# A fused attention and two-layer MoE kernel: the first token block's maximum is spread 14 instead of 4 scheduling steps behind the block's load

## The chip, the core and the metric

The kernel runs on one core of a Trainium2 chip. The core has five engines with a queue each: TensorE (PE in the profile, its weight loads PEld), VectorE (DVE), ScalarE (ACT), GpSimd (POOL) and SyncE (SP), which issues all the DMAs that matter here. Each engine works through its own queue in order and waits on semaphores for the others. The metric is the device time of one execution in microseconds (us), the median of several runs.

## What is computed

Attention with RMS-normalized q and k (batch 4, 12 heads, 448 tokens, head size 64), then two MLPs on the 1792 x 768 result:

```python
def _attn_ref(q, k, v, g_q, g_k):
    q_n, k_n = (rmsnorm(q, g_q), rmsnorm(k, g_k))
    scores = scale * np.matmul(q_n, k_n.transpose(0, 1, 3, 2))
    attn = softmax(scores)
    return np.matmul(attn, v)

def _moe_ref(x, w_in, w_out):            # 768 -> 2048 -> 768
    h = x @ w_in
    g = h * (1.0 / (1.0 + np.exp(-1.702 * h)))
    return g @ w_out

def _moe2_ref(x, w_in, w_out, alpha):    # 768 -> 2048 -> 768
    h = x @ w_in
    g = np.maximum(h, 0.0) + alpha * np.minimum(h, 0.0)
    return g @ w_out
```

(`softmax` stands for the reference's subtraction of the row maximum, exponential and division by the sum.) Large matmuls run as three float16 products of a high and a low half (high x high, high x low, low x high), so every operand is first scaled by a power of two into float16's range and then split in two by `split`: ScalarE writes the high half, VectorE the low half.

## The kernel before

The program has two layers. In the first, attention and the first MLP of the four batches b = 0 to 3 are interleaved. The last part of batch 3 is `moe1_out` (line 680): six output slices j of 128 rows, each one PSUM tile `yp` that 48 matmuls (line 689, 128x448) accumulate; ScalarE then copies it out (`y`, line 697) and SP stores it to `y_dram` (line 698). Below, one such run of 48 matmuls is called a **y group**. Its tiles come from the PSUM pool `ps_m` with three buffers, which small helpers also use.

While batch 3 runs, the generator `late_weights` (line 953) is advanced next to it: it loads and splits the second layer's input weights `w2i` (lines 963 to 966, with a last call of `weight_scales`, which spreads the weights' maximum over the partitions), then opens the pools of the second layer and calls `prepare(0)` (line 735). `prepare` works on a block of tokens, 512 for block 0, in two steps:

- first step: load the block of the first layer's output, `yr`, from `y_dram` (line 740), take each partition's largest absolute value on VectorE (`yone`, line 742), round it to a power of two (lines 104 and 105);
- second step: `partition_max` (line 114) makes a diagonal `diag` of these values (line 117), a single 128x128 matmul with a matrix of ones spreads them over the partitions (`pm`, line 119), VectorE takes the maximum (`my`, line 120); from it follow the scales `ysc` (line 752), the split of the block into its two halves `x2` (lines 124 and 125, six slices) and a factor `co` (line 757).

Between the two steps `late_weights` yields `P0` times (lines 971 and 972). The loop of lines 1097 to 1106 advances it once for a tick of `moe1` in the first 32 ticks, and twice for a tick after that; one y group has four ticks. What is left when the ticks are over is run out by `second_layer` (line 977) at its start. The yields thus decide which y groups are written ahead of the second step. A scheduler that orders by the written place then fixes each engine's queue.

`yr` lies in memory that the weights' staging tiles held, so its load waits for the last split of `w2i` on VectorE (line 164). Behind the y groups stand, on TensorE, the small matmul for `alpha`'s maximum (`partition_max` at line 726, tile `a`), and then the second layer's first product (line 774, `h`), which reads `x2` and `w2i`. The loads of the second layer's output weights (line 808) wait for the last y group, since they take over `g`'s memory.

Of the kernel before, what the change touches and what calls it, by code (L numbers as in the profile page):

```python
# [46 lines left out]
G1I = 1  # L47
G1O = 2
P1 = (2, 8)
P0 = 4  # L50
PAIR0 = 44
W2_RAW = 6
RSQRT_SEED = float(0x5F3759DF)
# [3 lines left out]
def attention_moe_kernel(  # L57
# [895 lines left out]
    def late_weights(ctx, att):  # L953
# [16 lines left out]
        next(first)  # L970
        for _ in range(P0):
            yield
# [165 lines left out]
```

## Time and profile before

| | us |
|---|---|
| median of 3 runs | 1230.93 (1230.83 to 1232.2) |
| the profiled execution | 1225.37 |
| its span, first to last instruction | 1223.6 |
| TensorE busy in it | 1088.8 |
| VectorE busy in it | 837.8 |
| ScalarE busy in it | 708.2 |

The page gives one profiled execution. Times in the trace count from the span's start. A busy TensorE is not TensorE at its peak, since its matmuls overlap; idle time in front of a matmul is a plainer sign, and the trace names what ended it. The granted TensorE clock stands as a share: 1.00 is 2.4 GHz, 0.50 is 1.2 GHz.

### The profile page before, as it was taken

Reading aid. Unit: us, or ns where it says so; the run is one execution under the profiler, and the core shown is the slowest. Engines: PE = TensorE matmul, PEld = TensorE weight load, DVE = VectorE, ACT = ScalarE, POOL = GpSimd, SP = SyncE. Lnnn points to the kernel's source line nnn. Section 1 sums busy time; section 2 is a strip of 40 time slices with the busy share of each in tenths; the row PEclk is TensorE's granted clock in tenths of the full one; section 3 lists DMA queues with packets and bytes.
Section 4 is the critical chain, followed back from the end, with each engine's and each line's share of the span. In section 5 each row is a group of like instructions: output and inputs, shape, how many; then the busy total and the mean of one; then the engine's idle time right before and its main releaser. Section 6 shows DMA issues by size and latency. Waiting matters only on the chain.

```text
span 1223.6 us, 18355 instructions
## 1 busy us (share of the span) xinstructions
PE 1088.8 (89%) x6685; PEld 616.3 (50%) x6685; DVE 837.8 (68%) x1602; ACT 708.2 (58%) x1465; POOL 79.4 (6%) x56
## 2 busy tenths in 40 slices
PE   0557698887999998999999998599999999999998
PEld 0334466665554444555555544244444467666665
DVE  7989888988656887466741858439896343787441
ACT  3656687888468687567852545126666444565220
POOL 0000000112311222020000000000000000000000
PEclk9968699999999999999999999799999999999999
DMA  8994446388678887666651821356524215353100
GB/s 205 248 263 139 112 130 166 68 169 145 145 153 155 140 168 151 146 131 119 121 102 47 312 73 50 118 191 221 204 88 155 78 65 165 94 166 108 55 33 33
DMA packets 300010, 166.11 MB, mean 136 GB/s; under 512 B 238736, under 2 KB 283280, under 8 KB 299920
## 3 DMA queue, kind: packets, MB, share of 16 engines
q1 hardware_dynamic: 299920, 164.95, 53.2%
q8 instruction: 52, 0.85, 0.3%
q14 instruction: 38, 0.31, 0.1%
HBM read 92.02 MB, written 25.69 MB: 96 GB/s over the span
## 4 chain that ended last, share of the span: by engine, by line
PE 55%; DVE 18%; DMA 12%; ACT 8%; issue 5%; SPq 3%; DVEq 0%; ACTq 0%
PE op L930 16%; PE yp L689 14%; PE hp L666 7%; PE h L774 7%; PE xp L516 5%; PE sp L438 3%; DVE ph L493 2%; DMA yr<-y_dram 2%; DMA g<-in_moe_w_in_dram 2%; PE tp L485 2%; DMA pt<-ph 2%; PE hp L619 1%; DMA t<-hl 1%; DVE g L125 1%; ACT pr L452 1%
## 5 line engine op out<-in xcount | busy, mean ns | idle before, releaser
L689 PE MATMUL yp<-g,w1o 128*128 128x448 f16 x1152 | 227.9, 357 | 0.6 <-DVE g L125 0.4
L774 PE MATMUL h<-x,w2i 128*128 128x512 f16 (+1 forms) x1152 | 219.3, 352 | 2.6 <-ACT neg L781 2.5
L666 PE MATMUL hp<-x,w1i 128*128 128x448 f16 x864 | 169.5, 353 | 4.4 <-DVE t L675 4.4
L774 PEld LDWEIGHTS <-w2i 128*128 128x128 f16 x1152 | 112.6, 98 | 108.1 <-issue 3.5
L689 PEld LDWEIGHTS <-w1o 128*128 128x128 f16 x1152 | 111.8, 99 | 109.6 <-issue 10.2
L666 PEld LDWEIGHTS <-w1i 128*128 128x128 f16 x864 | 82.9, 98 | 84.7 <-issue 8.9
L452 ACT ACTIVATE pr<-sp,nm,c_s 128x448 f32<-128x448 f32 x168 | 120.3, 720 | 2.5 <-PE tp L485 0.6
L493 DVE SCALAR_TENSOR_TENSOR ph<-pr,sm,ph 128x448 f16<-128x448 f32 x126 | 98.1, 805 | 20.4 <-ACT ph L470 19.5
L443 DVE TENSOR_REDUCE nm<-sp 128x2 f32<-128x896 f32 x96 | 92.7, 966 | 26.6 <-PE sp L438 26.3
L930 PEld LDWEIGHTS <-even 128*128 128x128 f16 x672 | 65.7, 98 | 43.1
L470 ACT ACTIVATE ph<-pr,sm 128x448 f16<-128x448 f32 x126 | 77.7, 659 | 12.9 <-DVE sm L461 9.6
L782 DVE SCALAR_TENSOR_TENSOR pos<-neg,nalpha,pos 128x512 f32<-128x512 f32 (+1 forms) x64 | 43.4, 679 | 60.0 <-ACT neg L781 59.8
L780 ACT ACTIVATE pos<-h 128x512 f32<-128x512 f32 (+1 forms) x64 | 34.4, 538 | 72.6 <-PE h L774 60.0
L619 PE MATMUL hp<-x,w1i 128*128 128x192 f16 (+1 forms) x576 | 60.3, 259 | 8.3 <-DVE t L631 3.9
L930 PEld LDWEIGHTS <-odd 128*128 128x128 f16 x504 | 49.3, 98 | 32.6
L438 PE MATMUL sp<-w1o 128*128 128x448 f16 (+1 forms) x64 | 21.4, 468 | 48.2 <-DMA w1o<-hl 31.5
L438 PE MATMUL sp<-t 128*128 128x448 f16 (+1 forms) x160 | 53.2, 377 | 12.2 <-ACT pr L452 8.1
L930 PE MATMUL op<-w2lo,even 128*128 128x384 f16 x384 | 63.5, 326 | 0.0
L444 ACT ACTIVATE nm<-nm,c_s 128x2 f32<-128x2 f32 x96 | 27.9, 291 | 56.2 <-DVE nm L443 55.9
L619 PEld LDWEIGHTS <-w1i 128*128 128x128 f16 x576 | 51.8, 98 | 16.3 <-issue 10.6
L485 PE MATMUL tp<-dg,pr 128*128 128x128 f32 x336 | 49.8, 301 | 10.3 <-DVE dg L465 7.6
L438 PE MATMUL sp<-t,t 128*128 128x448 f16 (+1 forms) x160 | 52.6, 374 | 6.7 <-DMA t<-t 6.7
(202 smaller groups left out, 1686.9 us busy)
## 6 DMA issues: line engine op xcount, KB each, us to landing
g<-in_moe_w_in_dram SPq DMA_DIRECT2D x24, 512.0 KB, 5.8
g<-in_moe_w_out_dram SPq DMA_DIRECT2D x32, 384.0 KB, 4.0
w2raw<-in_moe_w_in_dram SPq DMA_DIRECT2D x24, 512.0 KB, 5.6
w2raw<-in_moe_w_out_dram SPq DMA_DIRECT2D x16, 768.0 KB, 6.7
g_dram<-pos SPq DMA_DIRECT2D x48, 256.0 KB, 2.0
gp<-g_dram SPq DMA_DIRECT2D x8, 1024.0 KB, 7.4
odd<-g_dram SPq DMA_DIRECT2D x6, 1024.0 KB, 5.6
qk<-in_q_dram SPq DMA_DIRECT2D x24, 224.0 KB, 3.6
```

The lines of the kernel that those rows point to most:

```text
L438: nc.tensor.matmul(out=sp[rows, i, 0:S], lhsT=t1[:, c, rows], rhs=kt[:, j * S:(j + 1) * S], start=(e == 0), stop=(e == 1))
L443: nc.vector.tensor_reduce(out=nm[:, 0:n], in_=sp[:, 0:n, 0:S], op=ALU.max, axis=AX, negate=True)
L452: nc.scalar.activation(out=pr[i], in_=sp[:, i, 0:S], func=AF.Exp, bias=nm[:, i:i + 1], scale=c_s, accum_out=sm[:, i:i + 1])
L470: nc.scalar.activation(out=ph[:, i, 0:S], in_=pr[i], func=AF.Copy, scale=sm[:, i:i + 1])
L485: nc.tensor.matmul(out=tp[:, c, i], lhsT=pr[i][:, o:o + 128], rhs=ph[:, i], start=True, stop=True)
L493: nc.vector.scalar_tensor_tensor(out=ph[:, i, S:2 * S], in0=pr[i], scalar=sm[:, i:i + 1], in1=ph[:, i, 0:S], op0=ALU.mult, op1=ALU.subtract)
L516: nc.tensor.matmul(out=xp[64 * j:64 * j + 64, t:t + n], lhsT=vs[ks, c, j], rhs=pt[ks, kc, o:o + n], start=(i == 0), stop=(i == len(steps) ...
L619: nc.tensor.matmul(out=ps, lhsT=w1i[:, kk, e, m * 128:(m + 1) * 128], rhs=xs[0, kk][:, f, cols], start=(i == 0), stop=(i == 3 * KD - 1))
L666: nc.tensor.matmul(out=ps, lhsT=w1i[:, kk, e, m * 128:(m + 1) * 128], rhs=x[:, f], start=(n == 0), stop=(n == 3 * KD - 1))
L689: nc.tensor.matmul(out=ps, lhsT=w1o[:, m, e, j * 128:(j + 1) * 128], rhs=g[:, m, f], start=(n == 0), stop=(n == 3 * KF - 1))
L774: nc.tensor.matmul(out=ps, lhsT=w2i[:, kk, e, m * 128:(m + 1) * 128], rhs=x2[kk][:, f], start=(c == 0), stop=(c == 3 * KD - 1))
L930: nc.tensor.matmul(out=ps, lhsT=ops[:, o, m, f], rhs=rhs[:, e], start=(c == 0), stop=(c == 3 * KH - 1))
```

## The change

One number changes. The second step of `prepare(0)` is written ten more steps of `late_weights` later.

```diff
-P0 = 4
+P0 = 14
```

No instruction is added or removed. On TensorE's queue the place is the end of the `w2i` work and the middle of batch 3's y groups. In the names, `pm_7906` spreads the maximum of `w2i`, `pm_7954` that of token block 0, and `yp_7888` and `yp_7996` are two y groups. Before:

```order
L689 MATMUL yp_7888<-g_7233,w1o_78 128x448
L119 LDWEIGHTS ones_75 [waits DVE_49]
L119 MATMUL pm_7906<-diag_7904,ones_75 128x128 [waits Activation_49]
L119 LDWEIGHTS ones_75 [waits DVE_49]
L119 MATMUL pm_7954<-diag_7952,ones_75 128x128 [waits Activation_49]
L689 LDWEIGHTS w1o_78
L689 MATMUL yp_7996<-g_7233,w1o_78 128x448 [waits Activation_49]
```

The two small matmuls stand next to each other, and three y groups (144 matmuls) follow. With the change, at the same place of TensorE's queue, a y group (`yp_7966`) comes right behind the first small matmul:

```order
L689 MATMUL yp_7888<-g_7233,w1o_78 128x448
L119 LDWEIGHTS ones_75 [waits DVE_49]
L119 MATMUL pm_7906<-diag_7904,ones_75 128x128 [waits Activation_49]
L689 LDWEIGHTS w1o_78
L689 MATMUL yp_7966<-g_7233,w1o_78 128x448 [waits Activation_49]
```

and the small matmul of token block 0 (now `pm_8021`) stands behind that group's 48 matmuls, still on TensorE's queue:

```order
L689 MATMUL yp_7966<-g_7233,w1o_78 128x448
L119 LDWEIGHTS ones_75 [waits DVE_49]
L119 MATMUL pm_8021<-diag_8019,ones_75 128x128 [waits Activation_49]
L689 LDWEIGHTS w1o_78
L689 MATMUL yp_8048<-g_7233,w1o_78 128x448
```

So the small matmul has moved past one y group; two groups are left behind it instead of three. On ScalarE's queue the copy of that group (`y_8015`) has moved ahead of the six first halves of block 0, of which two are shown:

```order
L697 ACTIVATE y_7963<-yp_7888,c_y_99 128x448 [waits DMAHW7_49,PE_49,Activation_49]
L697 ACTIVATE y_8015<-yp_7966,c_y_99 128x448 [waits DMAHW0_49,PE_49,Activation_49]
L124 ACTIVATE x2_8028<-yr_7921,ysc_8026 128x512 [waits DMAHW2_49,DVE_49,Activation_49]
L124 ACTIVATE x2_8029<-yr_7921,ysc_8026 128x512
L124 ACTIVATE x2_8030<-yr_7921,ysc_8026 128x512
```

Before, that copy stood behind the six. On SP's queue the group's store has moved ahead of the load of token block 1 (`yr_8267`), behind that of block 0 (`yr_7921`):

```order
 L698 DMA y_dram_72<-y_7883 128x448 [waits Activation_49]
-L698 DMA y_dram_72<-y_7993 128x448 [waits DMAHW1_49,Activation_49]
+L698 DMA y_dram_72<-y_7963 128x448 [waits DMAHW1_49,Activation_49]
 L740 DMA yr_7921<-y_dram_72 128x6x512 [waits DMAHW4_49,DMAHW5_49,DMAHW3_49,DMAHW6_49,DMAHW2_49,DVE_49]
+L698 DMA y_dram_72<-y_8015 128x448 [waits Activation_49]
 L740 DMA yr_8267<-y_dram_72 128x6x512 [waits DMAHW2_49,DVE_49]
-L698 DMA y_dram_72<-y_8045 128x448 [waits Activation_49]
 L698 DMA y_dram_72<-y_8097 128x448 [waits Activation_49]
```

One store has passed one load there. VectorE's queue and GpSimd's have the same instructions in the same order, with other buffer numbers.

## Rows read from the trace of the kernel before

**Rows 1.** Page, part 1: busy us (share of span) and instructions by engine
```profile
PE 1088.8 (89%) x6685; PEld 616.3 (50%) x6685; DVE 837.8 (68%) x1602; ACT 708.2 (58%) x1465; POOL 79.4 (6%) x56
```

**Rows 2.** Waits of PE, whole span: us in total, times, longest
```profile
PE sp L438 <- DMA w1o<-hl: 31.5, 2, 27.4
PE pm L119 <- DVE diag L117: 19.7, 2, 16.8
```

**Rows 3.** Timeline, PE alone: start, us, engine line op, [idle before <-releaser]
```profile
61.81 4.88 PE L485 MATMUL tp<-dg,pr 128*128 128x128 f32 x24 [6.67 <-DVE dg L465]
...
760.31 0.22 PE L119 MATMUL pm<-diag,ones 128*128 128x128 bf16 x1
777.37 0.29 PE L119 MATMUL pm<-diag,ones 128*128 128x128 bf16 x1 [16.84 <-DVE diag L117]
777.45 30.01 PE L689 MATMUL yp<-g,w1o 128*128 128x448 f16 x144
807.30 0.22 PE L119 MATMUL pm<-diag,ones 128*128 128x128 bf16 x1
```

**Rows 4.** Timeline, ACT alone, 748 to 835 us
```profile
752.92 0.61 ACT L697 ACTIVATE y<-yp,c_y 128x448 f32<-128x448 f32 x1
...
763.72 0.61 ACT L697 ACTIVATE y<-yp,c_y 128x448 f32<-128x448 f32 x1
778.57 3.78 ACT L124 ACTIVATE x<-yr,ysc 128x512 f16<-128x512 f32 x6 [14.23 <-DVE ysc L752]
...
798.47 0.63 ACT L697 ACTIVATE y<-yp,c_y 128x448 f32<-128x448 f32 x1 [8.50 <-PE yp L689]
807.55 0.63 ACT L697 ACTIVATE y<-yp,c_y 128x448 f32<-128x448 f32 x1 [8.45 <-PE pm L119]
```

**Rows 5.** Timeline, all engines, 755 to 835 us: the chain of block 0
```profile
764.42 2.34 DVE L164 SCALAR_TENSOR_TENSOR w2i<-w2n,inv_w2i,w2i 128x2048 f16<-128x2048 f32 x1
...
766.79 16.99 SPq L740 DMA_DIRECT2D yr<-y_dram  x2
...
773.29 3.35 DVE L742 TENSOR_REDUCE yone<-yr 128x1 f32<-128x3072 f32 x1 [6.00 <-DMA yr<-y_dram]
...
777.05 0.25 DVE L117 TENSOR_SCALAR diag<-ident,yone 128x128 bf16<-128x128 bf16 x1
...
777.69 0.29 DVE L120 TENSOR_REDUCE my<-pm 128x1 f32<-128x128 f32 x1 [0.38 <-PE pm L119]
...
779.32 4.06 DVE L125 SCALAR_TENSOR_TENSOR x<-yr,ysc,x 128x512 f16<-128x512 f32 x6 [0.84 <-ACT x L124]
...
789.91 3.35 DVE L742 TENSOR_REDUCE yone<-yr 128x1 f32<-128x3072 f32 x1 [6.53 <-DMA yr<-y_dram]
...
807.76 0.24 DVE L117 TENSOR_SCALAR diag<-ident,yone 128x128 bf16<-128x128 bf16 x1
```

**Rows 6.** Busy time by stretch: us, each engine (instructions), PEclk, DMA share, GB/s
```profile
61.81:65.93 4.12, 4.12 (x19) 4.12 (x20) 4.12 (x11) 0.68 (x1) 0.00 (x0) 0.50 0.97 307
266.66:270.59 3.93, 0.00 (x0) 0.10 (x1) 3.93 (x8) 3.58 (x10) 0.00 (x0) 1.00 0.93 187
270.59:274.14 3.55, 3.55 (x26) 2.28 (x27) 3.55 (x10) 3.55 (x11) 1.05 (x1) 0.52 0.62 129
760.53:765.66 5.13, 0.00 (x0) 0.00 (x0) 3.71 (x3) 3.80 (x3) 0.00 (x0) 1.00 0.09 35
765.66:777.37 11.71, 0.01 (x1) 0.01 (x1) 5.47 (x8) 0.00 (x0) 0.00 (x0) 0.50 0.40 139
777.37:782.73 5.36, 5.36 (x16) 2.26 (x17) 4.20 (x11) 3.78 (x6) 0.00 (x0) 0.50 0.00 0
```

**Rows 7.** DMA issues, 762 to 775 us: count, KB each, median us to landing
```profile
yr<-y_dram SPq DMA_DIRECT2D x1, 1536.0 KB, 6.5
y_dram<-y SPq DMA_DIRECT2D x1, 224.0 KB, 1.9
```

**Rows 8.** Waits of PE, 807.6 us to the span's end
```profile
PE h L774 <- ACT neg L781: 2.5, 3, 1.7
```

## The prediction

> **What bounds the kernel now.** I read the engines' busy shares first: TensorE 89%, VectorE 68%, ScalarE 58% [rows 1]. TensorE is the engine to follow, but a share does not say where the time of one edit goes, so I went on to TensorE's waits. The largest is the start-up (27.4 us in one stop); the next largest single stop is 16.8 us, of the small matmul `pm` for the diagonal that VectorE makes [rows 2]. The timeline puts that stop at the edited place: the weights' `pm` ends at 760.31 + 0.22 = 760.53, block 0's `pm` starts at 777.37, and 144 matmuls of three y groups queue behind it [rows 3]. Those matmuls need nothing of block 0; they stand still only because TensorE's queue is in order.
>
> What ends the stop is block 0's chain, in the order of time [rows 5]: the last split of `w2i` ends at 766.76 and frees the staging memory; the load of `yr` is issued at 766.79 (the row merges it with block 1's load) and VectorE starts the maximum at 773.29; that takes 3.35, two small steps follow, and `diag` ends at 777.30. No step of this chain uses TensorE, so it is neither sped up nor held by what TensorE does meanwhile.
>
> Behind the y groups TensorE hardly waits: 2.5 us in the remaining 416 us of the span [rows 8]. So time gained on TensorE in this place should last to the end.
>
> **What the change moves, and its price.** Nothing is added or removed, and the small matmul passes one y group.
>
> *The y group in the hole.* A group at full clock is read from the copies of two successive groups, both of which wait for their group and start at 798.47 and 807.55 [rows 4]: 9.08 us. 144 matmuls took 30.01 [rows 3], where 3 x 9.08 = 27.24 would be the full-clock time; the surplus, 2.8 us, is the clock (below). The group can start right at 760.53: its PSUM tile is the one three requests back in a pool of three, whose copy ended at 752.92 + 0.61 = 753.53 [rows 4]. It then ends at 760.53 + 9.08 = 769.61. If it had to wait for the newer copy, which ends at 764.33 [rows 4], it would end at 773.4. Both are before 777.30, so the gain is the same: TensorE's stop shrinks from 16.84 to 7.76 us in the first case, `pm` stays at 777.37, and 96 matmuls are left behind it instead of 144. The gain is **9.08 us**.
>
> *The clock.* In the old stop the clock went from 1.00 to 0.50 at 765.66, 5.13 us into it, and after work resumed it stayed at 0.50 for 5.36 us [rows 6]. At half the rate that costs half of the stretch, 2.7 us, which agrees with the surplus of 2.8. Will a stop of 7.76 us still cost it? The two nearest stops are shorter, and both did: one of 6.67 us before 61.81 [rows 3] was followed by 4.12 us at 0.50, and one of 3.93 us before 270.59 [rows 6] by 3.55 us at 0.52. So the fall stays, and only its length varies: half of 3.55 to 5.36 us is 1.8 to 2.7. Against the 2.7 of now that is 0 to 0.9 us of further gain; I take 0, from the row of the same work (y groups), and keep 0.9 for the range.
>
> The Trainium skill, page "TensorE: Matmul & The Clock Gate" (section "Part 1: The HAM clock gate"), says that the number of slow matmuls at one place differs from run to run, and warns against fitting to one count. By it, the 5.36 us of this one execution are no fixed price and the clock term could come out somewhat longer too; no row here repeats the same place.
>
> *The group's copy.* On ScalarE it is now ahead of block 0's six first halves. It runs at about 769.6 for 0.6 us, in what was an idle stretch of 14.23 us before 778.57 [rows 4]; cost nothing. If the group ended only at 773.4 it would still fit.
>
> *The group's store.* SP issues it at about 770.3, behind block 0's load, which then is in flight until about 773.3. Before, no other transfer ran beside that load: the previous store could be issued when its copy had ended at 764.33 [rows 4], and landed in 1.9 us [rows 7]. If the two share the engines evenly, the load loses the store's share, 224 / 1536 x 6.5 = 0.95 us [rows 7], and `pm` and all behind it come that much later; if the store's packets wait their turn, nothing. Below nothing is excluded: a store does not speed a load. I take 0, since the load's packets were all queued 3.5 us earlier, and keep 0.95.
>
> The Trainium skill, page "DMA: Bandwidth & Descriptors" (section "Issuing engines are not separate DMA queues"), says that all DMAs run on the same 16 engines and interleave. By that rule the gain here would be 9.08 - 0.95 = 8.1 us instead of 9.1; no row of the kernel before has this pair in flight.
>
> *What SP's store passes.* Block 1's load stands behind it on SP and waits for block 0's split in any case, which ends at 783.38 [rows 5]; the store is issued 13 us before. No cost.
>
> *What is late next.* Block 0's split stays at 778.57 to 783.38 [rows 4, 5]. The last y group ends 9.1 us earlier, near 798.4; then come `alpha`'s small matmul and the second layer. Its inputs are there since 783.4. Block 1's `diag` waited behind `alpha`'s maximum until 807.76; its own maximum ended near 793.3 [rows 5], so it has 5 us to spare when everything moves up. The output weights' loads wait for the last y group, so they move up with it. Nothing becomes the new bound.
>
> **The sum.** Span 1223.6 - 9.1 = 1214.5; profiled execution 1225.37 - 9.1 = 1216.3. The median of the runs is 5.6 us above the profiled execution; I carry the difference over: 1230.93 - 9.1 = **1221.8 us**. With the bounds (0.95 lost, 0.9 gained) the forecast's own range is 1220.9 to 1222.8.
>
> **Rivals.**
> (a) The shorter stop does not drop the clock, and the surplus of 2.8 goes too: 9.1 + 2.8 = 11.9, 1219.0 us. For it: the stop is less than half as long. Against it: a stop of 3.93 us was enough [rows 6].
> (b) The gain is given back later, because the second layer's first 100 us hang on the output weights or on VectorE and not on TensorE: 1230.9. For it: VectorE is busy 68% overall [rows 1]. Against it: TensorE waits 2.5 us behind the place [rows 8], and the weights' loads move up as well.
> (c) Slower, by the clock: TensorE's busy time is now cut in two by the stop, and if the low level lasted through both remaining groups, 96 matmuls would take 4 x 9.08 = 36.3 us. From 760.53 on: 9.08 + 7.76 + 36.3 = 53.2, against 16.84 + 30.0 = 46.9 now: 6.3 us slower, 1237.2. It decides from a low stretch of 5.36 + 2 x 9.08 = 23.5 us on. Against it: the three low stretches after dense work resumed are 3.55, 4.12 and 5.36 us [rows 6].
> (d) The change does not do what it says, since the scheduler could have put the instructions where they were: excluded by the queues shown with the change, so I give it no chance.
>
> **How the numbers follow.** Forecast 0.84, (a) 0.05, (b) 0.05, (c) 0.02, and 0.04 for a part of the gain given back (1223.5 to 1228). A measurement of this kernel can tell about 0.2%, 2.5 us. Faster by more than that: the forecast, (a) and most of the partial case, 0.92; within 0.2%: (b) and the rest, 0.06; slower: 0.02. The range: the forecast's 1220.9 to 1222.8, widened by the 1.4 us that the three runs span, and down to (a): 1219.0 to 1224.2, which I round up to 1224.4.
>
> **What would show it.** In the profile of the changed kernel TensorE's wait for `diag` should be 7.8 us long (7 to 9); a y group of 9.1 us should lie directly behind the weights' `pm`; block 0's `pm` should start within 1 us of 777.4; the clock should read 0.50 for some 3.5 to 5.5 us behind it; block 0's load should land 6.5 to 7.4 us after its issue; `alpha`'s `pm` should start near 798.2 and everything behind it 9 us earlier than now, to the last store. Wrong would be: a `pm` that moves with the group (then the chain of block 0 does hang on TensorE), full clock behind the stop (a), or new waits of line 774 that eat the gain (b).

## The result, and the profile after

The changed kernel takes 1220.39 us (median of 4 runs, 1219.69 to 1220.57), the kernel before 1230.99 (4 runs, 1230.83 to 1232.2). By the medians that is 10.6 us faster. The ratio is 0.9911, 95% interval 0.9894 to 0.9928, or 11.0 us, between 8.9 and 13.0. Forecast were 1221.8 us, 9.1 us below, and a range of 1219.0 to 1224.4.

The profiled execution of the changed kernel took 1220.57 us with a span of 1218.8. That is only 4.8 us less than the span before; where the other 6 us are, the first experiment shows. First the edited place.

Timeline of the changed kernel, TensorE alone (start, duration, line and operation, idle time before and what ended it); it answers to [rows 3]:

```profile
766.44 0.23 PE L119 MATMUL pm<-diag,ones 128*128 128x128 bf16 x1 [0.57 <-DVE diag L117]
766.50 9.24 PE L689 MATMUL yp<-g,w1o 128*128 128x448 f16 x48
783.60 0.29 PE L119 MATMUL pm<-diag,ones 128*128 128x128 bf16 x1 [7.86 <-DVE diag L117]
783.68 20.24 PE L689 MATMUL yp<-g,w1o 128*128 128x448 f16 x96
803.76 0.22 PE L119 MATMUL pm<-diag,ones 128*128 128x128 bf16 x1
803.81 35.13 PE L774 MATMUL h<-x,w2i 128*128 128x512 f16 x162
```

The y group (48 matmuls) stands directly behind the weights' small matmul, the stop has shrunk from 16.84 to 7.86 us, and two groups (96 matmuls) are left behind it. The chain of block 0 in the same stretch, timeline of all engines, which answers to [rows 5]:

```profile
770.57 2.34 DVE L164 SCALAR_TENSOR_TENSOR w2i<-w2n,inv_w2i,w2i 128x2048 f16<-128x2048 f32 x1
...
772.94 0.37 SPq L740 DMA_DIRECT2D yr<-y_dram  x1
...
775.83 0.64 ACT L697 ACTIVATE y<-yp,c_y 128x448 f32<-128x448 f32 x1 [5.35 <-issue]
776.50 0.32 SPq L698 DMA_DIRECT2D y_dram<-y  x1
779.53 3.35 DVE L742 TENSOR_REDUCE yone<-yr 128x1 f32<-128x3072 f32 x1 [6.09 <-DMA yr<-y_dram]
...
783.29 0.25 DVE L117 TENSOR_SCALAR diag<-ident,yone 128x128 bf16<-128x128 bf16 x1
...
784.80 3.78 ACT L124 ACTIVATE x<-yr,ysc 128x512 f16<-128x512 f32 x6 [8.33 <-DVE ysc L752]
```

It runs as before, 6.1 to 6.2 us later as a whole. From the weights' small matmul to block 0's it is 783.60 - 766.44 = 17.16 us, before 777.37 - 760.31 = 17.06 [rows 3]. The moved copy (775.83) and the moved store (776.50) lie inside the chain's wait for its load. Busy time and clock by stretch (us, then PE, PEld, DVE, ACT, POOL busy with counts, PEclk, DMA share, GB/s), which answers to [rows 6]:

```profile
766.67:775.74 9.07, 9.07 (x48) 4.50 (x46) 5.27 (x6) 3.81 (x3) 0.00 (x0) 1.00 0.24 65
775.74:780.72 4.98, 0.01 (x1) 0.00 (x0) 1.19 (x1) 0.64 (x1) 0.00 (x0) 1.00 0.75 290
780.72:783.60 2.88, 0.00 (x0) 0.00 (x1) 2.72 (x4) 0.00 (x0) 0.00 (x0) 0.50 0.00 0
783.60:787.55 3.95, 3.95 (x12) 1.73 (x13) 2.78 (x8) 2.75 (x5) 0.00 (x0) 0.50 0.00 0
```

The group ran at full clock; the clock fell 4.98 us into the stop and stayed at 0.50 for 3.95 us after it, where it had stayed for 5.36. The wait of TensorE behind the place (807.6 us to the end before [rows 8], 804 us to the end now) and the two transfers that meet (KB, median us to landing; before [rows 7]) are:

```profile
PE h L774 <- ACT neg L781: 1.6, 1, 1.6
```

```profile
yr<-y_dram SPq DMA_DIRECT2D x1, 1536.0 KB, 6.6
y_dram<-y SPq DMA_DIRECT2D x1, 224.0 KB, 3.6
```

The stretch from the weights' small matmul to alpha's is 803.76 - 766.44 = 37.32 us against 807.30 - 760.31 = 46.99: 9.67 us gained. From alpha's small matmul to the end of the span it is 415.0 us against 416.3: another 1.3. That makes 11.0, near the measured 10.6. The stretch starts 6.1 us later (766.44 instead of 760.31), so the two spans differ by 4.8 us only.

### The profile page after: what moved, and what is told of

Its sections match the earlier page's. It is cut to its first block, busy times and chain, and to the rows that moved or that the text cites. A ratio compares the mean times of both kernels' runs of the same rounds, so it can differ in the third digit from the quotient of the medians.

```text
span 1218.8 us, 18355 instructions
## 1 busy us (share of the span) xinstructions
PE 1092.8 (90%) x6685; PEld 618.4 (51%) x6685; DVE 838.6 (69%) x1602; ACT 709.5 (58%) x1465; POOL 79.8 (7%) x56
## 4 chain that ended last, share of the span: by engine, by line
PE 54%; DVE 17%; DMA 13%; ACT 8%; issue 5%; SPq 3%; POOL 0%; ACTq 0%; DVEq 0%
PE op L930 16%; PE yp L689 13%; PE hp L666 7%; PE h L774 7%; PE xp L516 5%; PE sp L438 3%; DVE ph L493 2%; DMA qk<-in_q_dram 2%; DMA yr<-y_dram 2%; DMA w1o<-hl 2%; PE tp L485 2%; PE hp L619 2%; ACT pr L452 2%; DMA w2raw<-in_moe_w_in_dram 2%; DVE nm L443 1%
## 5 line engine op out<-in xcount | busy, mean ns | idle before, releaser
L493 DVE SCALAR_TENSOR_TENSOR ph<-pr,sm,ph 128x448 f16<-128x448 f32 x126 | 98.7, 810 | 19.1 <-ACT ph L470 18.2
L619 PE MATMUL hp<-x,w1i 128*128 128x192 f16 (+1 forms) x576 | 63.7, 268 | 8.3 <-DVE t L631 3.9
L619 PEld LDWEIGHTS <-w1i 128*128 128x128 f16 x576 | 53.5, 101 | 17.8 <-issue 10.6
```

Source lines behind the costliest of these rows:

```text
L493: nc.vector.scalar_tensor_tensor(out=ph[:, i, S:2 * S], in0=pr[i], scalar=sm[:, i:i + 1], in1=ph[:, i, 0:S], op0=ALU.mult, op1=ALU.subtract)
L619: nc.tensor.matmul(out=ps, lhsT=w1i[:, kk, e, m * 128:(m + 1) * 128], rhs=xs[0, kk][:, f, cols], start=(i == 0), stop=(i == 3 * KD - 1))
```

## The experiments

**The hole theory.** The chain of block 0 needs about 17.1 us from the weights' small matmul to block 0's, whatever TensorE does. What TensorE can do of the y groups in this time is the gain. The rest of the time it stands (the hole), and behind a long stop it pays for the low clock in addition. Its rivals: the gain comes from the clock; it comes from the first part of the program or from the second layer; or what was moved ahead of the chain stretches it.

All profiles together. "Weights' pm" is the start of that small matmul, "to block 0's pm" the chain, "stop" TensorE's idle time in front of the latter, "low clock" the time at 0.50 behind the stop, "to alpha's pm" the stretch in which the change lies, "rest" what follows up to the end of the span. All in us. Two rows are not like the others: with the useless fill ten matmuls of the fill stand ahead of the weights' small matmul, and with three groups alpha's small matmul stands right behind block 0's, ahead of the second layer's new wait.

| kernel | weights' pm | to block 0's pm | stop | low clock | to alpha's pm | rest |
|---|---|---|---|---|---|---|
| before | 760.31 | 17.06 | 16.84 | 5.36 | 46.99 | 416.3 |
| before, again | 762.29 | 17.12 | 16.90 | 6.02 | 47.38 | 415.5 |
| after | 766.44 | 17.16 | 7.86 | 3.95 | 37.32 | 415.0 |
| after, again | 760.48 | 16.81 | 7.51 | 5.13 | 37.54 | 415.7 |
| two groups | 766.08 | 18.22 | none | none | 27.35 | 413.1 |
| two groups, again | 762.64 | 18.22 | none | none | 27.36 | 413.1 |
| useless fill | 770.82 | 15.76 | 0.75 | none | 43.07 | 415.9 |
| three groups | 764.92 | 27.30 | none | none | 28.06 | 416.9 |

### The kernel before, profiled once more

No edit.

> The kernel before, unchanged, profiled once more. Question: the profile of the changed kernel reaches the weights' small matmul at 766.4 us, the one of before at 760.3, although the program up to there is the same. Theory A (executions differ in the first part by themselves): the matmul starts anywhere from 759 to 768 us here, while the stretch from it to alpha's small matmul is 46.5 to 47.9 us as before (46.99), with a stop of 16.7 to 17.0 us. Rival B (the change makes the first part 6 us longer and gives 6 us more back elsewhere): the matmul starts at 760 to 761 us again.

Timeline, TensorE alone, and the stretch at the low clock behind the stop:

```profile
762.29 0.22 PE L119 MATMUL pm<-diag,ones 128*128 128x128 bf16 x1
779.41 0.29 PE L119 MATMUL pm<-diag,ones 128*128 128x128 bf16 x1 [16.90 <-DVE diag L117]
779.49 30.34 PE L689 MATMUL yp<-g,w1o 128*128 128x448 f16 x144
809.67 0.22 PE L119 MATMUL pm<-diag,ones 128*128 128x128 bf16 x1
```

```profile
779.41:785.43 6.02, 6.02 (x17) 2.50 (x18) 4.85 (x11) 3.79 (x6) 0.00 (x0) 0.50 0.00 0
```

The weights' small matmul is at 762.29, 2 us later than in the first profile; the stretch is 47.38 us. So the part ahead of the edit differs by itself from execution to execution, and not in step with the edit: the changed kernel reached the place at 760.48 in its second profile, and all eight profiles, with the same order of instructions up to there, at 760.3 to 769.1 (the latest is the useless fill's, where the end of the y group ahead is the mark). Theory A holds. The spread comes early: the windows of the first 100 us show the clock at different levels on average, here in the kernel before (760.31), in the changed one (766.44) and in the changed one again (760.48):

```profile
0.00:100.00 100.00, 40.96 (x179) 23.22 (x180) 84.70 (x191) 51.91 (x100) 0.79 (x8) 0.85 0.91 232
```

```profile
0.00:100.00 100.00, 41.60 (x167) 22.80 (x168) 83.34 (x191) 50.82 (x97) 0.80 (x8) 0.83 0.88 226
```

```profile
0.00:100.00 100.00, 40.28 (x178) 23.23 (x179) 84.58 (x191) 51.85 (x99) 0.79 (x8) 0.88 0.89 231
```

In the late execution TensorE has got through 167 matmuls in that time, in the two early ones through 179 and 178, at a higher clock. It is not the whole of it: the execution with most, 184 at 0.88, is the second profile of the kernel before, and it came to the place at 762.29. That the clock is the cause was not tested; it may as well be the consequence of later loads. What follows for reading: spans of single executions can differ by up to 9 us here for this reason alone, so the spans cannot be compared, but the stretch between two marks can.

### The changed kernel once more

No edit; the times stand beside the experiments of the same chip.

> The changed kernel once more, for times beside the others and for a second look at the clock. Hole theory (a y group fills the stop, the chain of block 0 keeps its length): the stretch from the weights' small matmul to alpha's is 36.6 to 38.3 us, with a stop of 7.7 to 8.0 us; what varies is the low-clock stretch behind the stop, which was 3.95 us and was 5.36 in the kernel before. Time about 1220.4. Rival (the lower time comes from the first part or the second layer): the stretch differs from the first profile by more than 1 us while the time stays.

1219.12 us, ratio to the kernel before 0.9932 (0.9906 to 0.9958). Timeline of TensorE, the stretch behind the stop, and the two diagonals that VectorE makes for the weights and for block 0:

```profile
760.48 0.22 PE L119 MATMUL pm<-diag,ones 128*128 128x128 bf16 x1
760.53 9.24 PE L689 MATMUL yp<-g,w1o 128*128 128x448 f16 x48
777.29 0.29 PE L119 MATMUL pm<-diag,ones 128*128 128x128 bf16 x1 [7.51 <-DVE diag L117]
777.37 20.82 PE L689 MATMUL yp<-g,w1o 128*128 128x448 f16 x96
798.02 0.22 PE L119 MATMUL pm<-diag,ones 128*128 128x128 bf16 x1
```

```profile
777.29:782.42 5.13, 5.13 (x15) 2.21 (x16) 3.97 (x10) 3.78 (x6) 0.00 (x0) 0.50 0.00 0
```

```profile
759.59 0.25 DVE L117 TENSOR_SCALAR diag<-ident,wcol 128x128 bf16<-128x128 bf16 x1
776.98 0.25 DVE L117 TENSOR_SCALAR diag<-ident,yone 128x128 bf16<-128x128 bf16 x1
```

The stretch is 37.54 us, 0.2 from the first profile. The stop is 7.51, a little under what was expected (7.7 to 8.0). The 16.81 us from one small matmul to the other are not a shorter chain: TensorE was still in the y group ahead and came to the weights' small matmul 0.64 us after its diagonal was ready (759.84), in the first profile of the kernel before 0.07 us after. On VectorE alone, from the start of one diagonal to the start of the other, the chain took 17.39 us here and 17.03 to 17.27 in the seven other profiles. The low clock lasted 5.13 us against 3.95 in the first profile of the same kernel: its length at one and the same place is not fixed.

### Two groups in the hole

```diff
-P0 = 4
+P0 = 20
```

> P0 = 20: block 0's small matmul stands behind two y groups instead of one, one group is left behind it. Hole theory: the chain takes about 17.1 us from the weights' small matmul, two groups take 18.2, so there is no stop, the small matmul starts about 18.3 us after the weights' one, the clock stays at 1.00, and the stretch to alpha's small matmul is 3 x 9.1 + 0.4 = 27.6 us against 37.3 with one group and 47.0 with none: 19.4 us below the kernel before, about 1211.6 us. Block 0's split ends some 6 us behind its small matmul, 3 us before it is needed. Rival (the gain of one group came from the clock or from the second layer, not from the filled stop): 1218 to 1221 us. Rival (block 0's chain is stretched by the copies and stores that now come before it): a stop remains, its small matmul starts 19.5 us or more after the weights' one.

1208.23 us, ratio 0.9823 (0.9795 to 0.9850). Timeline of TensorE, and the busy time of the stretch up to block 0's small matmul:

```profile
766.08 0.22 PE L119 MATMUL pm<-diag,ones 128*128 128x128 bf16 x1
766.14 18.32 PE L689 MATMUL yp<-g,w1o 128*128 128x448 f16 x96
784.30 0.22 PE L119 MATMUL pm<-diag,ones 128*128 128x128 bf16 x1
784.36 9.24 PE L689 MATMUL yp<-g,w1o 128*128 128x448 f16 x48
793.43 0.22 PE L119 MATMUL pm<-diag,ones 128*128 128x128 bf16 x1
```

```profile
766.30:784.30 18.00, 18.00 (x98) 9.29 (x95) 9.18 (x10) 4.14 (x4) 0.00 (x0) 1.00 0.32 114
```

No stop, the clock at 1.00 throughout, 27.35 us to alpha's small matmul where 27.6 were expected. (The expected time, 1211.6 us, counted from the kernel before at 1231; measured beside this one it took 1227.87.) Block 0's small matmul comes 18.22 us after the weights' one, which is the two groups' length; `diag` was ready 1.6 us earlier (at 782.73):

```profile
782.48 0.25 DVE L117 TENSOR_SCALAR diag<-ident,yone 128x128 bf16<-128x128 bf16 x1
```

So the chain is not stretched by what now stands ahead of it. Of the two moved copies and stores only the first ran before `diag` (copy at 775.47, store at 776.13); the second copy ran at 784.55, behind the small matmul, and block 0's first halves, at 785.38, still waited for VectorE's `ysc` and not for it. And neither the clock alone nor the first part makes the gain. The stretch is 19.6 us shorter than before, and the rest of the program adds to it: it took 413.1 us instead of 415 to 416, and in it TensorE has no wait of the kind of [rows 8] left. Together some 22 us, within the ratio's interval (18.4 to 25.2 us). In this kernel the scheduler also puts VectorE's and ScalarE's work of the second layer in another order; whether that order or the earlier start removes the wait was not separated. The kernel with three groups (below) starts its second layer 1.7 us later than this one, in a third order, and has 2.1 us of this wait, so an early start alone is not enough.

### The hole filled with work of no use

The kernel before, with 101 matmuls ahead of block 0's small one. The first reads a scale of `w2i`, so that none can start before VectorE has made it; they write a PSUM tile that nothing reads. The lines that keep the scale in `invs` are left out here.

```diff
         for _ in range(P0):
             yield
+        fill = w2["ps"].tile([128, H2], F32, tag="op", name="fill")
+        nc.tensor.matmul(out=fill[0:12], lhsT=invs["w2i"].bitcast(BF16), rhs=w1o[:, 0, 0, 0:H2].bitcast(BF16), start=True, stop=True)
+        for i in range(100):
+            nc.tensor.matmul(out=fill, lhsT=w1o[:, i % KF, 0, 0:128], rhs=w1o[:, i % KF, 0, 0:H2], start=(i == 0), stop=(i == 99))
         next(first)
```

> The kernel before (P0 = 4) with 101 matmuls of 384 columns put ahead of block 0's small matmul; they read the first layer's output weights and write a PSUM tile that nothing reads. About 100 x 160 ns = 16 us, so the stop is filled with work of no use, and all three y groups still follow. Hole theory: nothing useful has moved, so only the clock's price comes back: the clock stays at 1.00, the stretch from the weights' small matmul to alpha's is about 44.3 us instead of 47.0, time 1228.2 us (2.0 to 3.5 below before). Rival (the clock makes most of the gain of the change): 1220 to 1224 us.

1227.45 us, ratio 0.9997 (0.9985 to 1.0010). Timeline of TensorE, and the busy time from the end of the y group ahead of the place:

```profile
770.82 0.22 PE L119 MATMUL pm<-diag,ones 128*128 128x128 bf16 x1
770.88 14.95 PE L976 MATMUL fill<-w1o 128*128 128x384 f16 x91
786.58 0.23 PE L119 MATMUL pm<-diag,ones 128*128 128x128 bf16 x1 [0.75 <-DVE diag L117]
786.65 27.40 PE L689 MATMUL yp<-g,w1o 128*128 128x448 f16 x144
813.89 0.22 PE L119 MATMUL pm<-diag,ones 128*128 128x128 bf16 x1
```

```profile
769.12:786.58 17.46, 16.71 (x102) 9.81 (x103) 9.44 (x11) 4.37 (x3) 0.00 (x0) 1.00 0.30 104
786.58:813.89 27.31, 27.31 (x146) 14.16 (x147) 8.51 (x14) 5.05 (x8) 0.00 (x0) 1.00 0.21 75
```

TensorE was busy nearly throughout, the clock stayed at 1.00, and the three y groups took 27.40 us instead of 30.01 [rows 3]: the clock's price is 2.6 us, close to the 2.7 to 2.8 that the prediction had read. Ten of the fill's matmuls stand ahead of the weights' small matmul, so here the end of the y group before is the mark: from it to alpha's small matmul 17.46 + 27.31 = 44.77 us. In the kernel before, that group is the end of this row:

```profile
739.69 20.78 PE L689 MATMUL yp<-g,w1o 128*128 128x448 f16 x109
```

It ended at 739.69 + 20.78 = 760.47, and 807.30 - 760.47 = 46.83. That is 2.1 us less and not 2.6, since block 0's small matmul came 0.6 us later after the mark (17.46 us instead of 16.90). In the whole time it does not show; the interval (1.8 us faster to 1.2 slower) ends just short of the 2.0 to 3.5 that were expected. The profiled execution came to the place later than any other; whether this kernel's other executions did so too, no profile shows, and where the 2 us went is open. The run does exclude the rival: a full hole and a full clock without useful work in it give nothing like 10 us.

### Three groups in the hole

```diff
-P0 = 4
+P0 = 36
```

> P0 = 36: block 0's small matmul stands behind all three y groups, none is left behind it. Hole theory: there is no stop in front of it (it starts 27.4 us after the weights' one), but now nothing covers the way from it to the first halves of block 0, which took 2.7 us (small matmul at 777.37, first pair of halves ready near 780.1): TensorE stops about 3 us in front of the second layer's first matmul. That matmul comes 30 to 31.5 us after the weights' small matmul, against 27.4 with two groups: 2.5 to 4 us slower than two groups in this stretch, still some 16 us below the kernel before. Rival (the later the small matmul the better): the first matmul of the second layer comes within 1 us of the 27.4 us of two groups.

1212.17 us, ratio 0.9850 (0.9817 to 0.9883). Timeline of TensorE:

```profile
764.92 0.22 PE L119 MATMUL pm<-diag,ones 128*128 128x128 bf16 x1
764.98 27.40 PE L689 MATMUL yp<-g,w1o 128*128 128x448 f16 x144
792.22 0.22 PE L119 MATMUL pm<-diag,ones 128*128 128x128 bf16 x1
792.98 0.23 PE L119 MATMUL pm<-diag,ones 128*128 128x128 bf16 x1 [0.55 <-DVE diag L117]
794.07 6.13 PE L774 MATMUL h<-x,w2i 128*128 128x512 f16 x27 [0.86 <-ACT x L124]
```

Block 0's small matmul is the one at 792.22, alpha's the one at 792.98. As expected a new wait appears in front of the second layer, on the halves of block 0 (`ACT x L124`), but it is smaller: the first matmul comes 29.15 us after the weights' small matmul, not 30 to 31.5, and 1.7 us later than with two groups (27.4). The expectation counted from the small matmul to the first pair of halves; the first matmul started at 794.07, right behind the first high half, which ScalarE wrote until 794.02, and before the low half, which VectorE wrote until 794.80; so 1.85 us sufficed. The rival (the later the better) is out as well.

Behind that first matmul three groups lose more: from it to the end of the span it is 415.8 us, with two groups 413.0. TensorE has 2.1 us of the wait of [rows 8] again, and VectorE's and ScalarE's work of the second layer stands in yet another order.

### Two groups, beside three

> P0 = 20 once more, on the chip and in the rounds of the kernel with three groups. Hole theory: 27.2 to 27.6 us from the weights' small matmul to the second layer's first matmul, no stop, clock 1.00; time 2 to 5 us below that of three groups, where the first part of the executions does not hide it. Rival (the first time of two groups was luck of the first part): less than 16 us below the kernel before.

1209.08 us, ratio 0.9823 (0.9786 to 0.9860); the kernel before, measured beside both, took 1231.74. The stretch is 27.36 us as in the other profile of this kernel:

```profile
762.64 0.22 PE L119 MATMUL pm<-diag,ones 128*128 128x128 bf16 x1
762.70 18.32 PE L689 MATMUL yp<-g,w1o 128*128 128x448 f16 x96
780.86 0.22 PE L119 MATMUL pm<-diag,ones 128*128 128x128 bf16 x1
...
790.00 0.22 PE L119 MATMUL pm<-diag,ones 128*128 128x128 bf16 x1
```

By the medians two groups are 3.1 us faster than three. By the profiles it is 1.7 up to the second layer's first matmul and 4.5 from the weights' small matmul to the end (440.4 against 445.0). The intervals of the two ratios overlap, so it is the profiles that carry the order. Both are well below the changed kernel (0.9932 and 0.9911).

## Why the prediction was right

Step by step, as it was put:

- **The chain does not use TensorE, so it keeps its length.** Right: 17.06 and 17.12 us before, 17.16 and 16.81 after; on VectorE alone, from diagonal to diagonal, 17.07 and 17.18 before, 17.16 and 17.39 after.
- **One y group fills 9.08 us of the stop, which becomes 7.76.** Right: the group ran from 766.67 to 775.74, 9.07 us at full clock, with a stop of 7.86 (7.51 in the second profile). Its PSUM tile was free; it started at once.
- **The clock falls all the same; 0 taken, up to 0.9 us of gain kept.** It fell. The low stretch was 3.95 and 5.13 us, against 5.36 and 6.02 before, so half of the difference, 0.4 to 0.7 us, came on top in the pairs taken in order. The price of the whole fall, read as 2.7 to 2.8 us, was confirmed apart from everything else: 2.6 us with the useless fill. The Trainium skill, page "TensorE: Matmul & The Clock Gate" (section "Part 1: The HAM clock gate"), says of a kernel's start that the count of slow matmuls differs from run to run. The traces show the same behind this stop: 12 and 15 TensorE instructions ran in the low stretch of the changed kernel's two profiles, 3.95 and 5.13 us.
- **The moved store: 0 taken, up to 0.95 us of loss kept.** Right: the load took 6.6 instead of 6.5 us. Over all profiles it took 6.4 to 6.8 us with such a store behind it (five) and 6.5 to 6.6 without (three), so no loss stands out. The store paid instead, 3.6 us to land instead of 1.9, and nobody waits for it. Its packets waited their turn, the case for which the prediction had put down no loss: by 778.40, 1.90 us after the store's issue, 708 of the load's 768 packets of 2048 bytes had started and none of the store's 128 of 1792 bytes. The Trainium skill, page "DMA: Bandwidth & Descriptors" (section "Issuing engines are not separate DMA queues"), says that DMAs run on the same 16 engines and interleave. The trace shows the two interleaved only from 778.40 to 779.05, and the 8.1 us of gain that the prediction had worked out for even sharing did not come.
- **The moved copy costs nothing.** Right: it ran at 775.83 within ScalarE's idle time.
- **Behind the place the gain lasts.** Right, with 1.3 us more from the second layer in the first pair of profiles (416.3 to 415.0). With the second pair (415.5 and 415.7) that is within what repeated executions differ by.
- **Rivals.** (a), the clock stays up, and (c), it stays down for over 23 us, did not come; (b), the gain given back in the second layer, neither. The time alone could not have told the forecast from (a): 1220.39 lies midway between their 1221.8 and 1219.0. The 0.50 behind the stop told them apart.
- **The signs.** In the second profile block 0's `pm` started at 777.29 and alpha's at 798.02, as forecast (777.4 and 798.2). In the first they started at 783.60 and 803.76, 6 us later. A `pm` that moves with the group had been named as a sign of being wrong; it did not move with the group, since the weights' `pm` ahead of both was 6.1 us later as well. What the prediction had wrong there was to take one execution's time of arrival at the place for a fixed one, and so its profiled execution of 1216.3 us too: 1220.57 and 1215.47 were measured. The forecast of the median rests on the gain alone and was not touched by it.

The sum had 9.1 us; the stretch gave 9.67 in the first pair of profiles and 47.38 - 37.54 = 9.84 in the second. What was left out is the clock's variable part in the first pair (0.7, less 0.1 for the chain), and in the second 0.45 of the clock and 0.3 because TensorE came to the weights' small matmul late, with part of the chain already run. The median moved by 10.6 us; measured beside the experiments, the ratio 0.9932 (0.9906 to 0.9958) of 1227.87 us is 8.3, from 5.2 to 11.5. The 1.4 us by which the forecast of 1221.8 missed lie within that.

What the prediction did not ask is whether one group is the right number. Its own numbers held the answer: the chain takes 17.1 us, two groups 18.2, and the way from block 0's small matmul to the second layer's first matmul is covered by the third.

## What to carry to other kernels

When an in-order engine waits for a chain that it takes no part in, count how much independent work stands behind the waiting instruction and move just so much ahead of it that the chain is covered; here one group of three recovered 9.7 us, two 19.6, and the third, by leaving nothing to cover the next wait, lost 1.7 again (and 2.8 more in the second layer, whose order had changed). Read such an edit between two marks that enclose it, not from the span: the stretch repeated within 0.4 us, while its start moved by up to 9 us between executions. And before giving a slow clock the credit or the blame, price it alone by filling the stop with work of no use: here 2.6 us of a stop of 16.8.

## What was not expected of the hardware

A store issued 3.56 to 4.41 us behind a load of 1536 KB on the same queue did not slow it by more than loads differ anyway (6.4 to 6.8 us with such a store, 6.5 to 6.6 without) and was itself 2.9 to 3.6 us under way instead of 1.9: its packets started when nearly all of the load's had. The length of the low-clock stretch behind a stop varied at one place from 3.95 to 5.13 us in one kernel (stops of 7.86 and 7.51 us) and from 5.36 to 6.02 in the other (16.84 and 16.90); whether it grows with the stop, two profiles each cannot say. And the first part of the program, with an unchanged instruction order, reached the edited place between 760.3 and 769.1 us; its cause is open.
